# First operands made by engines alone, second pair loaded at the start, PE turning the identity meanwhile: an LSH attention and mixture-of-experts kernel on one core

## The chip, the cores and the metric

The kernel runs on one core of a Trainium2 chip. The metric is device time in microseconds (us) of one launch, as the median of several runs. The engines are named as the profile names them: PE (TensorE; PEld is its weight load), DVE (VectorE), ACT (ScalarE), POOL (GpSimd), and SP, whose queue issues most DMAs.

## What is computed

Inputs are q, k, v of 4 batches x 8 heads x 768 tokens x 64, a projection of 64 x 6, and the weights of 8 experts. Attention runs only inside a hash bucket; the rest of the kernel is a top-1 mixture of experts on the 3072 x 512 result.

```python
q_bits = (np.einsum('bhsd,dk->bhsk', q, proj) > 0)     # 6 sign bits per row; k likewise
mask = q_bucket[:, :, :, None] == k_bucket[:, :, None, :]
scores = np.where(mask, scale * np.matmul(q, k.transpose(0, 1, 3, 2)), -1000000000.0)
attn = np.exp(scores - max); attn = attn / (attn.sum + 1e-09)
x = np.matmul(attn, v)                                  # heads side by side: 3072 x 512
...
h = np.maximum(x[mask] @ w1[e], 0.0); ye = h @ w2[e]    # for the expert e with the largest logit
out[mask] = gate_w * sigmoid(x @ w_output_gate)[e] * ye
```

## The kernel before

Heads go in 16 pairs. A pair takes 12 steps, a step is one tile of 128 query rows of one head against all 768 keys, so there are 192 steps. `scores` (L476) does eight matmul rows per step: xl against xr (128 deep) and yl against yr (76 deep), each in two halves of 384 keys, into one of two PSUM buffers `ps_s`. The four operand tiles of a head hold a rounded value, its remainder, and the 12 sign bits that make the mask: xl and xr the rounded q and k with k's remainder, yl q's remainder and query bits, yr rounded k and key bits. DVE copies the masked scores out with their minimum (L488), ACT takes the exponential (`soft`, L496), DVE inverts the row sum (L503, L504), POOL scales (`normal`, L506), PE turns the result (`transposed`, L517), ACT copies it out (L518) and PE multiplies by v (`weighted`, L528).

The order on PE, DVE, ACT and POOL is the order of the code. Steps go in groups of two; a step's scaling comes two steps later, its transposes four, its products from step 10 on. The lists `at` and `products` hang extra work on steps: `plan(step, fn)`.

What makes the operands differs by pair. For the later pairs, `project` (L386) makes four small matmuls on the pair's two `qk` tiles and one DVE comparison into `bt`; `split_hi` (L430, POOL) rounds, `split_lo` (L438, DVE) takes remainders, and `spread` (L446) has SP issue eight DMAs per head that copy halves of these tiles between partitions: xr and yr from xl, xr from yl, xl from xl, and the bits from `bt` into yr and yl. For the first pair, head 0 is made by engines (`first_head`, L399), and head 1 by `project(0, (1,))`, `split_hi`, `split_lo` and `spread(..., True)`, whose large copies go to ACT and POOL and whose bits go by DMA. The projection operand `pjc` comes from `pj` by four small DVE instructions (L89, L90).

Before the first step the code issues: the two loads of pair 0, the identity (POOL), head 0, head 1, the first load of pair 1, the second, the load of v, and `more_constants` (L123), a list of 29 small POOL instructions and one DMA. Pair 1's `project` is planned for step 4, `split_hi` for steps 3 and 5, `split_lo` for 5 to 8, `spread` for 6 and 8. There are two buffers for `qk`. `tile_of` (L470) takes the three tiles of one head and then of the other in steps 0 to 5, and alternates heads afterwards.

After step 191 the kernel runs the experts, with PE as the busiest engine; nothing there is touched by the change.

Of the kernel before, what the change touches and what calls it, by code (L numbers as in the profile page):

```python
# [20 lines left out]
NB = 6  # L21
# [23 lines left out]
GROUP = 2  # L45
NFB = F // P
# [12 lines left out]
def lsh_attention_then_moe(  # L59
# [21 lines left out]
    pj = cst.tile([P, NB + 5], F32, name="pj")  # L81
    nc.scalar.dma_start(pj, proj)
    thr, scl, thr0, scl0, sgn = (pj[:, NB + i:NB + i + 1] for i in range(5))
    pjc = cst.tile([P, 32 + 2 * NB], F32, name="pjc")
    nc.vector.memset(pjc, 0.0)
    for h, s in ((0, 1.0), (1, -1.0)):
        hs = slice(h * D, (h + 1) * D)
        c = 2 * NB * h
        nc.vector.tensor_scalar(pjc[hs, c:c + NB], pj[hs, 0:NB], s, None, ALU.mult)  # L89
        nc.vector.tensor_scalar(pjc[hs, c + NB:c + 2 * NB], pj[hs, 0:NB], -s, None, ALU.mult)  # L90
# [32 lines left out]
    def more_constants():  # L123

        nc.gpsimd.memset(wgt, 0.0)
        nc.sync.dma_start(wgt[:, :, 0:2 * E], wgo.rearrange("(g p) c -> p g c", p=P))

# [6 lines left out]
        for ti, tf, pattern, first, cm in iotas:  # L134
            nc.gpsimd.iota(ti, pattern=pattern, base=first, channel_multiplier=cm)
            nc.gpsimd.tensor_copy(tf, ti)
        nc.gpsimd.memset(base, 0.0)
        for i, c in enumerate(CAPS):
            nc.gpsimd.memset(caps[:, i:i + 1], float(c))
        nc.gpsimd.memset(tacc_e, 0.0)  # L140
        for a in range(NB32):
            nc.gpsimd.memset(quart[32 * a:32 * a + 32], float(a))

# [209 lines left out]
    with ExitStack() as actx:  # L353
# [32 lines left out]
        def project(g, heads=(0, 1)):  # L386
            st = pairs[g]
            pp = ps_m.tile([P, HS], F32, name="ps_m")
            for j in heads:
                for n in range(2):  # L390
                    r = 32 * (2 * j + n)
                    nc.tensor.matmul(pp[r:r + 32], pjc[:, 0:32], st["qk"][j][:, n * HS:(n + 1) * HS],
                                     start=True, stop=True)
            bt = hp.tile([P, HS], F32R, name="bt", bufs=2)
            hs = slice(heads[0] * D, (heads[-1] + 1) * D)
            nc.vector.tensor_scalar(bt[hs], pp[hs], thr[hs], scl[hs], ALU.is_gt, ALU.mult)
            st["bt"] = bt

        def first_head():  # L399

            st = pairs[0]
            qk = st["qk"][0]
            xl, xr = (hp.tile([P, S], F32R, name=n) for n in ("xl", "xr"))
            yl = hp.tile([P, S], F32R, name="yl")
            yr = hp.tile([D + 2 * NB, S], F32R, name="yr")
            for k, t in (("xl", xl), ("yl", yl), ("xr", xr), ("yr", yr)):
                st[k] = [t, None]
            pp = ps_m.tile([P, HS], F32, name="ps_m")
            for m in range(2):
                ms = slice(m * D, (m + 1) * D)  # L410
                for n in range(2):
                    r = 32 * (2 * m + n)
                    nc.tensor.matmul(pp[r:r + 32], pjc[ms, 2 * NB * m:2 * NB * m + 32], qk[ms, n * HS:(n + 1) * HS],
                                     start=True, stop=True)
            nc.scalar.copy(xr[D:P], qk[D:P])
            nc.gpsimd.tensor_scalar(xr[0:D], qk[D:P], 1.0, 0.0, ALU.mult, ALU.add)
            nc.scalar.activation(xl[0:D], qk[0:D], AF.Copy, scale=-0.125)
            nc.vector.tensor_tensor(xr[D:P], qk[D:P], f32(xr[D:P]), ALU.subtract)
            nc.scalar.activation(xl[D:P], qk[0:D], AF.Copy, scale=-0.125)
            nc.gpsimd.tensor_scalar(yr[0:D], qk[D:P], 1.0, 0.0, ALU.mult, ALU.add)  # L420
            bt = hp.tile([P, HS], F32R, name="bt", bufs=2)
            nc.vector.tensor_scalar(bt, pp, thr0, scl0, ALU.is_gt, ALU.mult)
            nc.vector.scalar_tensor_tensor(yl[0:D], qk[0:D], -0.125, f32(xl[0:D]), ALU.mult, ALU.subtract)
            for n in range(2):
                cs = slice(n * HS, (n + 1) * HS)
                nc.gpsimd.tensor_scalar(yr[D:D + 2 * NB, cs], f32(bt[D + 32 * n:D + 32 * n + 2 * NB]), 1.0, 0.0,
                                        ALU.mult, ALU.add)
                nc.scalar.copy(yl[D:D + 2 * NB, cs], f32(bt[32 * n:32 * n + 2 * NB]))

        def split_hi(g, j):  # L430
# [3 lines left out]
            xl = hp.tile([P, S], F32R, name="xl")  # L434
# [11 lines left out]
        def spread(g, j, hurry=False):  # L446
# [5 lines left out]
            if hurry:  # L452
                qk = st["qk"][j]
                for t in ("xr", "yr"):
                    nc.scalar.copy(st[t][j][0:D], qk[D:P])
                nc.gpsimd.tensor_scalar(st["xr"][j][D:P], yl[D:P], 1.0, 0.0, ALU.mult, ALU.add)
                nc.scalar.activation(st["xl"][j][D:P], qk[0:D], AF.Copy, scale=-0.125)
            else:
                nc.sync.dma_start(xr[0:D], xl[D:P])
                nc.sync.dma_start(yr[0:D], xl[D:P])  # L460
                nc.sync.dma_start(xr[D:P], yl[D:P])
# [599 lines left out]
```

## Time and profile before

| | |
|---|---|
| median of 3 runs | 802.86 us (801.79 to 804.91) |
| the profiled execution | 803.36 us |
| its span, first to last instruction | 801.6 us |
| PE busy | 776.2 us, 97% |
| DVE, ACT, POOL busy | 59%, 57%, 47% |
| mean granted PE clock | 0.992 |

The profile describes one execution; 1.76 us of its time lie outside the span. Busy PE time is modelled from matmul ends, so a busy PE is not a PE at its peak. A row of the timeline has start, duration, engine, line, operation, result and sources, shape, count, and in brackets the idle time of that engine before it with what ended it.

### The profile page before, as it was taken

The page shows a single profiled execution, that of the slowest core. Times are in us where ns is not written, and L with a number is a line of the kernel's source. Part 1 is how long each engine was busy: PE and PEld are TensorE (multiplying, and loading weights), DVE is VectorE, ACT ScalarE, POOL GpSimd, SP SyncE. Part 2 cuts the span into 40 slices and gives each one's busy share as a digit, 9 for nine tenths or more (in the row PEclk, how much of TensorE's full clock was granted, in tenths as well). Part 3 has the DMA queues.
Part 4 walks back from the last instruction along what each step waited for, and adds up shares of the span by engine and source line. Part 5 has one row for each costly group of instructions (what it writes and reads, how often), then busy time and mean ns, then how long its engine had stood idle before and what let it go on. Part 6 is the DMA issues. An engine that isn't in the chain of part 4 may idle for free. (4 is left out here: it accounts for less than half of the span.)

```text
span 801.6 us, 13652 instructions
## 1 busy us (share of the span) xinstructions
PE 776.2 (97%) x4656; PEld 606.2 (76%) x4656; DVE 472.6 (59%) x1036; ACT 459.1 (57%) x934; POOL 375.9 (47%) x415
## 2 busy tenths in 40 slices
PE   6899999999999999999999999999999999999997
PEld 3666776667676667676667668888899999998895
DVE  5566676687666677667777546345444546454640
ACT  5767777657777667777677761144242525352331
POOL 5535444434534344544446864363617372746101
PEclk9999999999999999999999999999999999999999
DMA  3543645544655444564465512364444444444601
GB/s 123 127 110 77 146 89 127 135 97 91 144 125 103 105 127 81 125 145 87 110 154 145 146 28 67 132 202 152 148 131 154 151 151 148 147 150 164 226 27 38
DMA packets 84895, 98.94 MB, mean 123 GB/s; under 512 B 58047, under 2 KB 59535, under 8 KB 84816
## 3 DMA queue, kind: packets, MB, share of 16 engines
q1 hardware_dynamic: 79472, 84.66, 40.5%
q0 software_dynamic: 5200, 13.31, 4.9%
q8 instruction: 39, 0.64, 0.3%
q14 instruction: 40, 0.33, 0.1%
q10 hardware_dynamic: 144, 0.01, 0.0%
HBM read 59.48 MB, written 13.11 MB: 91 GB/s over the span
## 5 line engine op out<-in xcount | busy, mean ns | idle before, releaser
L506 POOL TENSOR_SCALAR sc<-sc,rsum 128x768 f32<-128x768 f32 x192 | 179.8, 948 | 234.6 <-DVE rsum L504 127.9
L488 DVE TENSOR_SCALAR_CACHE_REDUCE sc<-ps_s 128x768 f32<-128x768 f32 x192 | 183.4, 956 | 115.0 <-PE ps_s L484 105.9
L518 ACT COPY pts<-ps_t 128x384 f32<-128x384 f32 x384 | 164.3, 480 | 99.2 <-PE ps_t L517 98.6
L496 ACT ACTIVATE sc<-sc,mn 128x768 f32<-128x768 f32 x192 | 181.3, 944 | 25.2 <-DVE sc L488 16.2
L517 PE MATMUL ps_t<-ident,sc 128*128 128x128 f32 x1152 | 159.3, 274 | 4.9 <-POOL sc L506 2.4
L517 PEld LDWEIGHTS ps_t<-ident,sc 128*128 128x128 f32 x1152 | 136.7, 141 | 18.0 <-issue 6.7
L528 PE MATMUL ps_a<-pts,vt 128*64 128x384 f32 x768 | 148.6, 510 | 0.0
L484 PE MATMUL ps_s<-xr,xl 128*128 128x384 f32 x384 | 119.5, 393 | 5.2 <-DVE sc L488 3.3
L484 PEld LDWEIGHTS ps_s<-xr,xl 128*128 128x128 f32 x384 | 59.5, 195 | 78.5 <-issue 36.3
L484 PE MATMUL ps_s<-yr,yl 76*128 76x384 f32 x384 | 101.8, 347 | 0.2 <-issue 0.2
L297 PE MATMUL ps_s<-xh,w1h 128*128 128x256 f32 (+7 forms) x288 | 97.3, 338 | 2.1 <-DVE hl L308 1.6
L308 DVE SCALAR_TENSOR_TENSOR hl<-ps_s,hh 128x256 fp32r<-128x256 f32 (+8 forms) x40 | 34.0, 849 | 110.8 <-ACT hh L307 110.8
L297 PE MATMUL ps_s<-xlo,w1h 128*128 128x256 f32 (+7 forms) x288 | 95.4, 331 | 0.0
L297 PE MATMUL ps_s<-xh,w1l 128*128 128x256 f32 (+7 forms) x288 | 95.3, 331 | 0.0
L271 POOL DMA_INDIRECT xq<-x_dram,idx x75 | 81.6, 1088 | 21.6 <-issue 21.0
L528 PEld LDWEIGHTS ps_a<-pts,vt 128*64 128x64 f32 x768 | 47.5, 138 | 51.9 <-issue 50.1
L314 POOL DMA_INDIRECT out_dram<-yo,sid x29 | 30.6, 1057 | 115.3 <-ACT yo L313 61.3
L307 ACT ACTIVATE hh<-ps_s 128x256 fp32r<-128x256 f32 (+8 forms) x40 | 29.0, 726 | 92.8 <-PE ps_s L297 92.8
L484 PEld LDWEIGHTS ps_s<-yr,yl 76*128 76x128 f32 x384 | 72.0, 194 | 0.7 <-issue 0.5
L297 PEld LDWEIGHTS ps_s<-xh,w1h 128*128 128x128 f32 x288 | 54.2, 188 | 5.1 <-DVE hl L308 2.1
L297 PEld LDWEIGHTS ps_s<-xlo,w1h 128*128 128x128 f32 x288 | 54.2, 188 | 1.1
L297 PEld LDWEIGHTS ps_s<-xh,w1l 128*128 128x128 f32 x288 | 54.2, 188 | 1.1
(199 smaller groups left out, 1000.5 us busy)
## 6 DMA issues: line engine op xcount, KB each, us to landing
w_raw<-in_w_dram SPq DMA_DIRECT2D x36, 512.0 KB
qk<-in_qkT_dram SPq DMA_DIRECT2D x32, 384.0 KB
xh<-in_w_dram SPq DMA_DIRECT2D x14, 512.0 KB
xlo<-in_w_dram SPq DMA_DIRECT2D x14, 512.0 KB
vt<-in_v_dram SPq DMA_DIRECT2D x16, 384.0 KB
xr<-xl SPq DMA_DIRECT2D x30, 192.0 KB
yr<-xl SPq DMA_DIRECT2D x30, 192.0 KB
xr<-yl SPq DMA_DIRECT2D x30, 192.0 KB
```

Of the source, the lines that this page charges most:

```text
L271: nc.gpsimd.indirect_dma_start(out=xq[:, k * P:(k + 1) * P], out_offset=None, in_=x_dram.rearrange("n (a f) -> (n a) f", a=NB32), in_offse ...
L297: nc.tensor.matmul(ps, l, r, start=first and k == 0, stop=last and k == len(pairs) - 1)
L307: nc.scalar.activation(hh, ph, AF.Relu)
L308: return lambda: nc.vector.scalar_tensor_tensor(hl, ph, 0.0, f32(hh), ALU.max, ALU.subtract)
L314: nc.gpsimd.indirect_dma_start(out=out[:, :], out_offset=bass.IndirectOffsetOnAxis(ap=sid[0:n, r, a:a + 1], axis=0), in_=yo[0:n], in_offse ...
L484: nc.tensor.matmul(ss[:, n, 0:HS], l[0:k, qs], r[0:k, n * HS:(n + 1) * HS], start=first, stop=not first)
L488: nc.vector.tensor_scalar(sc, ss[:, :, 0:HS], MASKED, None, ALU.min, ALU.min, accum_out=mn)
L496: nc.scalar.activation(pr, pr, AF.Exp, bias=mn, scale=-1.0, accum_out=sums[s // GROUP][:, k:k + 1])
L506: nc.gpsimd.tensor_scalar(live[s0 + k], live[s0 + k], rs[:, k:k + 1], 0.0, ALU.mult, ALU.add)
L517: nc.tensor.transpose(tr[:, c], pr[:, (3 * h + c) * P:(3 * h + c + 1) * P], ident)
L518: nc.scalar.copy(pts[:, 3 * h:3 * h + 3, t * P:(t + 1) * P], tr)
L528: nc.tensor.matmul(st["av"][j * D:(j + 1) * D], st["v"][:, j, c], blocks[hb][j][:, c], start=(c == 0), stop=(c == NT - 1))
```

## The change

- `first_head` becomes `first_heads`: both heads of pair 0 are projected straight from `pj` (which now carries the projection twice, padded to 32 columns), each into its own PSUM tile, and all operands are made on POOL, ACT and DVE. No DMA carries bits for pair 0. The remainders of head 1 (`first_low`: four DVE instructions and one on POOL) stand after step 0, as do the four small instructions that make `pjc` (`signed`), now on POOL.
- Pair 1's two loads and the first load of v are issued at the start, and there are four `qk` buffers. Pair 1's project, split and spread come one step earlier. Steps 12 to 17 also take one head's three tiles and then the other's.
- PE turns the identity 14 times into a `ps_t` tile before its first projection.
- `more_constants` is cut into ten parts, planned for steps 18, 20, ... 36.

```diff
-    pj = cst.tile([P, NB + 5], F32, name="pj")
+    pj = cst.tile([P, 32 + 4], F32, name="pj")
...
-    def more_constants():
+    def gate_weights():
         nc.gpsimd.memset(wgt, 0.0)
         nc.sync.dma_start(wgt[:, :, 0:2 * E], wgo.rearrange("(g p) c -> p g c", p=P))
...
+    def more_constants():
+        return [gate_weights, triangle] + [lambda i=i: numbers(*i) for i in iotas] + [counters, tables]
...
-                t = hp.tile([P, S], F32, name="qk", bufs=2)
+                t = hp.tile([P, S], F32, name="qk", bufs=4)
...
+            pps = [ps_m.tile([P, HS], F32, name="ps_m"), ps_a.tile([P, HS], F32, name="ps_a")]
+            for j in range(2):
+                project_bits(j, pps[j])
+            nc.scalar.copy(xr[0][D:P], qk[0][D:P])
+            round_to(xr[0][0:D], qk[0][D:P])
+            nc.scalar.activation(xl[0][0:D], qk[0][0:D], AF.Copy, scale=-0.125)
+            nc.vector.tensor_tensor(xr[0][D:P], qk[0][D:P], f32(xr[0][D:P]), ALU.subtract)
+            nc.scalar.activation(xl[0][D:P], qk[0][0:D], AF.Copy, scale=-0.125)
+            round_to(yr[0][0:D], qk[0][D:P])
+            set_bits(pps[0])
+            split_hi(0, 1, xl[1])
+            nc.vector.scalar_tensor_tensor(yl[0][0:D], qk[0][0:D], -0.125, f32(xl[0][0:D]), ALU.mult, ALU.subtract)
+            key_bits(0)
+            query_bits(0)
+            set_bits(pps[1])
+            round_to(xr[1][0:D], qk[1][D:P])
+            key_bits(1)
+            query_bits(1)
+            nc.scalar.copy(yr[1][0:D], qk[1][D:P])
...
-            t, j = (i % 3, i // 3) if s < 6 else (i // 2, i % 2)
+            t, j = (i % 3, i // 3) if s // 6 in (0, 2) else (i // 2, i % 2)
...
-                s0 += 2 * (g == 1)
+                s0 += g == 1
...
+        for i, fn in enumerate(more_constants()):
+            plan(18 + 2 * i, fn)
...
             load(0)
+            load(1)
+            load_v(0)
             make_identity(nc, ident)
-            first_head()
-            project(0, (1,))
-            split_hi(0, 1)
-            split_lo(0, 1, 0)
-            split_lo(0, 1, 1)
-            load(1, (0,))
-            spread(0, 1, True)
-            load(1, (1,))
-            load_v(0)
-            more_constants()
+            warm = ps_t.tile([P, 3, P], F32, name="ps_t")
+            for i in range(NWARM):
+                nc.tensor.transpose(warm[:, i % 3], ident, ident)
+            first_heads()
...
+                    if s == 0:
+                        first_low()
+                        signed()
```

The order of POOL before, from pair 0's key bits on (`bt` holds the bits, `sc` is a step's scaled tile):

```order
L426 TENSOR_SCALAR yr<-bt 12x384 x2
L435 TENSOR_SCALAR xl<-qk,pj 128x768
L456 TENSOR_SCALAR xr<-yl 64x768
L125 MEMSET wgt 128x128
L129 MEMSET t_ob 128x128
L130 AFFINE_SELECT t_ob<-t_ob 128x128
L132 CAST tri<-t_ob 128x128
```

The same place in the change, with the lines numbered by the new code (L552 is `normal`):

```order
L439 TENSOR_SCALAR yr<-bt 12x384 x2
L449 TENSOR_SCALAR xr<-qk 64x768
L439 TENSOR_SCALAR yr<-bt 12x384 x2
L480 TENSOR_SCALAR xl<-qk 64x768
L93 TENSOR_SCALAR pjc<-pj 64x6
L94 TENSOR_SCALAR pjc<-pj 64x6
L552 TENSOR_SCALAR sc<-sc,rsum 128x768 x2
L488 TENSOR_SCALAR xl<-qk,pj 128x768
```

The rounding of head 1 now stands ahead of these rows, and the first scaling follows without the constants between.

The order of SP's queue before, from its start (L379 loads qk, L461 and L462 copy parts of pair 1's operands):

```order
L379 DMA qk<-in_qkT_dram 128x768 x2
L384 DMA vt<-in_v_dram 128x768 x2
L466 DMA yr<-bt 12x384
L379 DMA qk<-in_qkT_dram 128x768
L466 DMA yr<-bt 12x384
L467 DMA yl<-bt 12x384 x2
L379 DMA qk<-in_qkT_dram 128x768
L126 DMA wgt<-in_wgo_dram 128x4x16
L459 DMA xr<-xl 64x768
L460 DMA yr<-xl 64x768
L466 DMA yr<-bt 12x384 x2
```

And in the change, from its start:

```order
L394 DMA qk<-in_qkT_dram 128x768 x4
L399 DMA vt<-in_v_dram 128x768 x2
L394 DMA qk<-in_qkT_dram 128x768 x2
L512 DMA yr<-bt 12x384
L505 DMA xr<-xl 64x768
L506 DMA yr<-xl 64x768
L512 DMA yr<-bt 12x384
L507 DMA xr<-yl 64x768
L508 DMA xl<-xl 64x768
L505 DMA xr<-xl 64x768
L513 DMA yl<-bt 12x384 x2
```

The loads of pairs 0, 1 and 2 now all stand ahead of pair 1's copies; before, pair 2's loads stood among them.

## Rows read from the trace of the kernel before

**Rows 1.** The page's busy times: PE.
```profile
PE 776.2 (97%) x4656; PEld 606.2 (76%) x4656; DVE 472.6 (59%) x1036; ACT 459.1 (57%) x934; POOL 375.9 (47%) x415
```

**Rows 2.** Stretches: bounds, length, busy time of each engine, granted PE clock, DMA share, GB/s.
```profile
10.08:21.95 11.87, 10.20 (x36) 7.19 (x35) 7.07 (x17) 7.83 (x15) 9.63 (x39) 1.00 0.28 75
21.95:31.97 10.02, 9.59 (x63) 8.31 (x60) 8.94 (x20) 8.05 (x20) 5.20 (x6) 1.00 0.61 146
31.97:49.05 17.08, 14.95 (x85) 8.82 (x83) 7.59 (x20) 10.94 (x26) 7.35 (x9) 0.90 0.37 88
49.05:53.42 4.37, 4.37 (x30) 3.16 (x29) 4.06 (x11) 3.16 (x9) 1.91 (x2) 1.00 0.62 128
...
24.04:33.83 9.79, 9.25 (x64) 7.61 (x62) 9.28 (x23) 9.79 (x23) 4.68 (x5) 1.00 0.57 148
```

**Rows 3.** Timeline of PE, 0 to 25 us.
```profile
5.47 2.41 PE L413 MATMUL ps_m<-qk,pjc 64*32 64x384 f32 x8 [5.47 <-DVE pjc L90]
...
19.04 1.54 PE L517 MATMUL ps_t<-ident,sc 128*128 128x128 f32 x6 [1.03 <-POOL sc L506]
20.51 1.51 PE L392 MATMUL ps_m<-qk,pjc 128*32 128x384 f32 x8
21.95 1.01 PE L484 MATMUL ps_s<-xr,xl 128*128 128x384 f32 x2
...
23.40 0.78 PE L517 MATMUL ps_t<-ident,sc 128*128 128x128 f32 x5
...
24.04 0.60 PE L484 MATMUL ps_s<-xr,xl 128*128 128x384 f32 x2
...
24.83 0.82 PE L517 MATMUL ps_t<-ident,sc 128*128 128x128 f32 x6
```

**Rows 4.** Timeline of DVE, 4 to 13 us.
```profile
4.62 0.74 DVE L89 TENSOR_SCALAR pjc<-pj 64x6 f32<-64x6 f32 x1 [3.63 <-DMA pj<-in_proj_dram]
...
7.93 0.68 DVE L422 TENSOR_SCALAR bt<-ps_m,pj 128x384 fp32r<-128x384 f32 x1 [0.73 <-PE ps_m L413]
...
11.46 1.15 DVE L443 SCALAR_TENSOR_TENSOR yl<-qk,pj,xl 128x384 fp32r<-128x384 f32 x2 [0.57 <-POOL xl L435]
12.64 0.96 DVE L488 TENSOR_SCALAR_CACHE_REDUCE sc<-ps_s 128x768 f32<-128x768 f32 x1
```

**Rows 5.** POOL: timeline to 20 us, between it L426's instructions (ns min/median/max).
```profile
1.08 0.29 POOL masks.py:199 TENSOR_SCALAR_AFFINE_SELECT ident<-ident 128x128 f32<-128x128 f32 x1
...
L426 POOL TENSOR_SCALAR yr<-bt x2: 508/828/1147, 8.7 to 9.9; 12x384 fp32r<-12x384 f32 x2
...
13.65 0.20 POOL L125 MEMSET wgt<- 128x128 f32 x1
...
14.67 0.20 POOL L133 MEMSET ones<- 128x128 bf16 x1
...
17.50 0.48 POOL L142 MEMSET quart<- 32x1 f32 x4
18.08 1.79 POOL L506 TENSOR_SCALAR sc<-sc,rsum 128x768 f32<-128x768 f32 x2
```

**Rows 6.** Timeline of SP's queue and PE, 35 to 46 us.
```profile
35.79 0.47 SPq L462 DMA_DIRECT2D xl<-xl  x1
...
38.74 0.58 PE L484 MATMUL ps_s<-xr,xl 128*128 128x384 f32 x2 [1.84 <-DMA xl<-xl]
...
40.71 2.83 PE L528 MATMUL ps_a<-pts,vt 128*64 128x384 f32 x8
...
45.27 0.85 PE L392 MATMUL ps_m<-qk,pjc 128*32 128x384 f32 x8
```

**Rows 7.** Timeline of POOL, 55 to 58 us.
```profile
55.87 1.98 POOL L506 TENSOR_SCALAR sc<-sc,rsum 128x768 f32<-128x768 f32 x2 [2.38 <-PE ps_s L484]
```

**Rows 8.** Two later stretches, columns as in rows 2.
```profile
150.00:175.00 25.00, 23.50 (x148) 15.66 (x145) 20.61 (x61) 15.19 (x37) 10.10 (x10) 0.93 0.43 89
...
275.00:300.00 25.00, 23.50 (x147) 15.55 (x145) 20.55 (x61) 15.43 (x35) 10.27 (x11) 0.93 0.41 104
```

More of the change, by code (lines that the diff above doesn't have):

```diff
@@ L133, in more_constants, with numbers, counters @@
         nc.gpsimd.memset(ones, 1.0)
-        for ti, tf, pattern, first, cm in iotas:
-            nc.gpsimd.iota(ti, pattern=pattern, base=first, channel_multiplier=cm)
-            nc.gpsimd.tensor_copy(tf, ti)
+    def numbers(ti, tf, pattern, first, cm):
+        nc.gpsimd.iota(ti, pattern=pattern, base=first, channel_multiplier=cm)
+        nc.gpsimd.tensor_copy(tf, ti)
+    def counters():
         nc.gpsimd.memset(base, 0.0)
@@ L393, in project, with first_heads @@
                                      start=True, stop=True)
             bt = hp.tile([P, HS], F32R, name="bt", bufs=2)
-            hs = slice(heads[0] * D, (heads[-1] + 1) * D)
-            nc.vector.tensor_scalar(bt[hs], pp[hs], thr[hs], scl[hs], ALU.is_gt, ALU.mult)
+            nc.vector.tensor_scalar(bt, pp, thr, scl, ALU.is_gt, ALU.mult)
             st["bt"] = bt
-        def first_head():
+        def first_heads():
             st = pairs[0]
[L402 to L410, printed above, removed]
-                for n in range(2):
[L412 to L423, printed above, removed]
@@ new lines, in first_heads, with project_bits @@
+            qk = st["qk"]
+            for k in ("xl", "yl", "xr"):
+                st[k] = [hp.tile([P, S], F32R, name=k) for _ in range(2)]
+            st["yr"] = [hp.tile([D + 2 * NB, S], F32R, name="yr") for _ in range(2)]
+            xl, yl, xr, yr = (st[k] for k in ("xl", "yl", "xr", "yr"))
+            bits = []
+            def project_bits(j, pp):
+                for m in range(2):
+                    ms = slice(m * D, (m + 1) * D)
+                    for n in range(2):
+                        r = 32 * (2 * m + n)
+                        nc.tensor.matmul(pp[r:r + 32], pj[ms, 0:32], qk[j][ms, n * HS:(n + 1) * HS],
+                                         start=True, stop=True)
@@ new lines, in set_bits, with key_bits @@
+            def set_bits(pp):
+                bt = hp.tile([P, HS], F32R, name="bt", bufs=2)
+                nc.vector.tensor_scalar(bt, pp, 0.0, set0, ALU.is_gt, ALU.is_equal)
+                bits.append(f32(bt))
+            def key_bits(j):
+                for n in range(2):
+                    r = D + 32 * n
+                    nc.gpsimd.tensor_scalar(yr[j][D:D + 2 * NB, n * HS:(n + 1) * HS], bits[j][r:r + 2 * NB], 1.0, 0.0,
+                                            ALU.mult, ALU.add)
@@ new lines, in query_bits, with round_to @@
+            def query_bits(j):
+                for n in range(2):
+                    r = 32 * n
+                    nc.scalar.activation(yl[j][D:D + 2 * NB, n * HS:(n + 1) * HS], bits[j][r:r + 2 * NB], AF.Copy,
+                                         scale=PEN)
+            def round_to(dst, src):
+                nc.gpsimd.tensor_scalar(dst, src, 1.0, 0.0, ALU.mult, ALU.add)
+            pps = [ps_m.tile([P, HS], F32, name="ps_m"), ps_a.tile([P, HS], F32, name="ps_a")]
+            for j in range(2):
+                project_bits(j, pps[j])
@@ L433, in split_hi @@
                 st.setdefault(k, [None, None])
[L434 removed]
+            if xl is None:
+                xl = hp.tile([P, S], F32R, name="xl")
             nc.gpsimd.tensor_scalar(xl, st["qk"][j], sgn, 0.0, ALU.mult, ALU.add)
@@ L451, in spread @@
             xr, yr = f32(st["xr"][j]), f32(st["yr"][j])
[L452 to L461, printed above, removed]
-                nc.sync.dma_start(xl[D:P], xl[0:D])
+            nc.sync.dma_start(xr[0:D], xl[D:P])
+            nc.sync.dma_start(yr[0:D], xl[D:P])
+            nc.sync.dma_start(xr[D:P], yl[D:P])
+            nc.sync.dma_start(xl[D:P], xl[0:D])
             for n in range(2):
```

46 lines of the change are left out of this document (26 added, 20 removed).

## The prediction, written before the changed kernel was timed

> **What bounds the kernel now.** I read the page's busy times first: PE is busy for 776 us, 97% of the span [rows 1]. So a change off PE gains only where PE waits, or runs slowly. I then cut the span into stretches at places where PE begins the scores of a certain step, counting the score rows on PE's timeline: step 0 at 10.08, step 5 at 21.95, step 11 at 31.97, step 16 at 49.05 us [rows 2, 3]. From step 16 on two steps take 4.37 us with PE full [rows 2]. That is the pace of the rest of the attention, so what happens after step 16 only moves with it, and the question is how much earlier step 16 begins. Three stretches come before it.
>
> *Start to step 5.* PE waits until 5.47 us for DVE's preparation of `pjc` [rows 3], which itself waited until 4.62 for the small load of `pj` [rows 4]. POOL's list of constants runs from 13.65 to about 17.98, and the first scaling begins right behind it at 18.08 [rows 5]; PE had waited 1.03 us for that at 19.04 [rows 3]. And PE runs slowly here. The clock column prints 1.00 [rows 2], but the durations contradict it: a score pair takes 1.01 us at 21.95 and 0.60 us at 24.04; six transposes take 1.54 us at 19.04 and 0.82 us at 24.83 [rows 3]. [...]
>
> *Steps 5 to 11.* Six steps in 10.02 us, 1.67 each [rows 2]. ACT is busy for all of 24.04 to 33.83 (9.79 of 9.79 us) [rows 2]: with no products yet, ACT's exponential and copies set the pace, not PE.
>
> *Steps 11 to 16.* 17.08 us for five steps [rows 2]. PE waits 1.84 us at 38.74 for the copy `xl<-xl` of pair 1, issued only at 35.79 [rows 6]; then the granted clock falls (0.90 over the stretch [rows 2]) and eight product rows take 2.83 us [rows 6].
>
> **The change, part by part.** The sum is made against the profiled execution, 803.36 us (span 801.6 and 1.76 around it); it lies 0.50 us above the median of the runs.
>
> *Step 5.* The projections no longer wait for `pjc`: they need `pj` (4.62, [rows 4]) and PE, which has turned the identity 14 times. POOL has made the identity by 1.08 + 0.29 = 1.4 us [rows 5], and one transpose at the low level is 1.54/6 = 0.26 us [rows 3], so PE is free at 1.4 + 14 x 0.26 = 5.0. These transposes cost nothing of their own but 0.4 us: `pj` isn't there before 4.62. Head 0's projection (1.5 us, as at 20.51 [rows 3]) ends at about 6.6, the comparison (0.68, [rows 4]) at 7.3. The key bits on POOL come next: the two such instructions lasted 0.51 and 1.15 us [rows 5], so they end between 8.4 and 9.6; I take 8.9. Step 0's scores then finish at about 9.5, and DVE copies them out from 9.6, 3.0 us earlier than at 12.64 [rows 4]. Most of that is given back at once: `first_low` puts four half-tile DVE instructions behind it, 4 x 1.15/2 = 2.3 us by the nearest row [rows 4], so step 1's copy begins at 9.6 + 0.9 + 2.3 = 12.8 and ends at 13.7, which frees the buffer for step 3's scores. `first_low`'s own results are needed for step 3 as well, so both come in time together. The POOL rounding `xl` and the four small `pjc` instructions follow beside step 2; the first scaling after them. With the constants gone it is bound by the row sum, after step 2's copy (about 15.0), and done at 15.9. PE from 13.8: scores of step 3, pair 1's projection, scores of step 4, transposes of step 0, then step 5. At the high level, from start to next start, a score step is 24.83 - 24.04 = 0.79, a projection nearly the 0.85 of 45.27 [rows 6], six transposes some 0.6 (0.82 with the last one's tail [rows 3]): 0.8 + 0.8 + 0.8 + 0.6 = 3.0, so step 5 begins at 16.8. At the low level these are 1.45 (21.95 to 23.40), 1.45 (20.51 to 21.95), 1.45 and 1.47 (19.04 to 20.51) [rows 3]: 5.8, and step 5 at 19.6. Against 21.95 that is a gain of 5.1 or of 2.3 us. I take 5.0: PE is busy without a gap from 1.4 to about 8, longer than the gapless stretch from 19.04 that ended in the rise at 23.4, and slow scores before step 2 cost little, since DVE sets that part.
>
> [...] The trace shows the rise at 23.4 after a gapless run of transposes, projection and scores from 19.04 [rows 3], so it can't say which of them brought it. [...]
>
> *Steps 5 to 11.* ACT's work per step is unchanged, so 10.0 us again. Gain 0.
>
> *Steps 11 to 16.* Pair 1's tiles are loaded at the start, so the splits wait for nothing but their turn, and SP's queue has no load of pair 2 between the copies (it stands ahead, and needs only pair 0's buffers, free by about 14). The last remainder of head 0 follows step 5's copy, at about 19.5; its copies and bits, two DMA hops that each took up to 2.95 us before (35.79 to 38.74, [rows 6]) plus issues, end near 26.5, and step 12 begins near 30.2. Head 1's come some 4 to 5 us later, and the new tile order asks for them only at step 15, near 36. So both waits go. Without them: the first step with products 3.3 us (1.67 for a step and two products at some 1.44 to 1.5), then two groups at 4.37 [rows 2], and pair 2's projection, 0.8: 12.8 us. The gain is 17.1 - 12.8 = 4.3, with the slow stretch after the wait included. If head 1's copies were late by as much as one such wait, 1.84 us [rows 6], it would be 2.5.
>
> *Costs moved later.* The ten parts of the constants take 4.3 us of POOL together, the largest (`triangle`) 13.8 to 14.9, 1.1 us [rows 5]. POOL idles 2.38 us before each scaling in the steady steps [rows 7], waiting for others; with a `split_hi` of 0.9 in the same group the largest part still fits. I cost it at nothing; if that cover were gone, the whole of it is 4.3 us. The gate weights' DMA waits for a POOL instruction of step 18, with pair 2's last copies behind it on SP; those are needed from step 24, some 13 us later. Nothing. More loads at the start (six of 384 KB instead of four) stand behind pair 0's own in the queue, and the small load of `pj` met a busy queue before too; 0 to 0.5 us, and I take 0.
>
> Sum: 5.0 + 0 + 4.3 = 9.3 less 0.1 for the unknowns above, 9.2 us: 803.36 - 9.2 = **794.2 us**, 8.7 below the median of the runs. The bounds of the terms (2.3 to 5.1, and 2.5 to 4.3, and key bits 0.5 either way) give gains of 4.5 to 10, so its own range is 792.5 to 797.
>
> **The rivals.**
> - *The clock stays low, or falls again, until step 5.* For: no row shows the clock rise behind transposes alone [rows 3], and PE still waits from about 10.5 to 13.7 for `first_low` and step 1's copy, 3 us, where before a wait of 1.84 us with little work around it was followed by the low clock [rows 6]. Against: 6.5 us of gapless work. Gain 2.3 + 4.3 = 6.6: 796.8 us. [...]
> - *The change does not bring pair 1 in time.* The DMA copies still follow one another in pairs on one queue, with larger loads in flight. If head 0 or head 1 stalls as before, only step 5's gain is left: 803.4 - 4.6 = 798.8. Against: 4 us of slack for either head by the working above.
> - *Later slow stretches fall away.* At 150 to 175 and 275 to 300 us the clock averages 0.93 over 25 us [rows 8]: 25 x 0.07 x 2 = 3.5 us at half speed, 1.75 us lost each. PE waits there anyway, and all moves 9 us earlier; if the clock didn't follow those waits this time, both losses go: 794.2 - 3.5 = 790.7. A third such stretch would as well add 1.75.
> - *Slower than before.* The ten constant parts sit in steps 18 to 36, where PE has no slack. Should a part stand ahead of a scaling that PE waits for, PE waits and the clock falls after it, 1.75 us each as just worked out. Ten times that and the 4.3 us of the parts are 21.8 us: 794.2 + 21.8 = 816. It decides where a part is longer than POOL's idle time, 2.38 us less 0.9 in a group with a split [rows 7]; the longest is 1.1. So it is unlikely.
>
> **How the numbers follow.** Forecast 0.55, low clock 0.22, pair 1 late 0.08, later slow stretches gone 0.12, slower 0.03. From 790.5 to 798 all cases but the third, the last and some tails of the rest are held, about 8 in 10. A measurement of this kernel tells about 0.5%, 4.0 us, from no change, so faster means under 798.8: the first, second and fourth case and half of the third, 0.93; no change 0.04; slower 0.03.
>
> **What would show it.** In the changed profile: PE busy from about 1.4 us with 14 transposes of some 0.26 us, the first scores at about 8 us; step 1's copy on DVE behind the four `first_low` instructions near 12.8; the first scaling near 15.0; step 5 at 16.8 (19.6 with the low clock); ACT full between steps 5 and 11; no wait of PE on `xl<-xl` or `yl<-bt` at steps 12 to 15; step 16 near 39.8; then 4.37 us per two steps. The prediction is wrong if step 16 comes after 44, if PE's scores at step 12 or 15 wait for a DMA, if PE waits for POOL in steps 20 to 40, or if the attention's later pace changes.

## The result, and the profile after

The changed kernel takes 799.03 us as the median of 11 runs (796.41 to 799.68), the kernel before 802.86 us beside it (11 runs, 799.76 to 804.91). The ratio is 0.9949, 95% interval 0.9934 to 0.9964. That is a gain of 3.8 us, where 8.7 were forecast and the range, 790.5 to 798 us, began at 4.9: the prediction is **wrong in size**, right in sign. Three of the eleven runs took 796.4 to 797.0 us at a mean granted clock of 0.992 to 0.995, the other eight 798.7 to 799.7 at 0.986 to 0.990; the profiled execution is one of the eight (799.08 us, span 797.4). Against the profile before it gains 803.36 - 799.08 = 4.28 us.

The page's busy times of the changed kernel (before: [rows 1]):

```profile
PE 772.7 (97%) x4674; PEld 606.8 (76%) x4674; DVE 472.4 (59%) x1034; ACT 458.4 (57%) x934; POOL 383.4 (48%) x422
```

Its stretches between the same steps (step 0 to 5, 5 to 11, 11 to 16, 16 to 18), columns as in [rows 2], where the four that answer to these stand:

```profile
6.81:19.96 13.15, 9.62 (x35) 6.48 (x35) 8.88 (x18) 6.95 (x14) 9.09 (x14) 0.61 0.34 116
19.96:30.20 10.24, 9.10 (x63) 7.58 (x62) 10.01 (x24) 9.76 (x23) 7.01 (x7) 1.00 0.56 128
30.20:43.19 12.99, 12.87 (x85) 8.25 (x84) 7.27 (x18) 10.83 (x26) 7.18 (x9) 1.00 0.50 128
43.19:47.55 4.36, 4.36 (x30) 3.18 (x28) 4.06 (x11) 3.15 (x9) 1.91 (x2) 1.00 0.51 106
```

The reader sees three things. Steps 11 to 16 shrank from 17.08 to 12.99 us, at a clock of 1.00 instead of 0.90. Steps 5 to 11 kept their length. But step 5 begins at 19.96 instead of 21.95, and the clock of the first stretch is 0.61. PE's timeline tells why (start, duration, operation; in brackets the idle time before and what ended it):

```profile
1.43 3.25 PE L833 MATMUL ps_t<-ident 128*128 128x128 f32 x14 [1.43 <-POOL ident masks.py:199]
4.61 1.45 PE L428 MATMUL ps_m<-qk,pj 64*32 64x384 f32 x8
5.89 0.82 PE L428 MATMUL ps_a<-qk,pj 64*32 64x384 f32 x8
6.81 0.58 PE L530 MATMUL ps_s<-xr,xl 128*128 128x384 f32 x2
9.03 1.28 PE L530 MATMUL ps_s<-yr,yl 76*128 76x384 f32 x2 [1.65 <-POOL yr L439]
10.11 0.84 PE L530 MATMUL ps_s<-xr,xl 128*128 128x384 f32 x2
...
14.80 0.98 PE L530 MATMUL ps_s<-xr,xl 128*128 128x384 f32 x2 [1.78 <-DVE sc L534]
...
16.35 1.51 PE L407 MATMUL ps_m<-qk,pjc 128*32 128x384 f32 x8
17.79 1.01 PE L530 MATMUL ps_s<-xr,xl 128*128 128x384 f32 x2
...
19.24 0.96 PE L563 MATMUL ps_t<-ident,sc 128*128 128x128 f32 x6
19.96 0.60 PE L530 MATMUL ps_s<-xr,xl 128*128 128x384 f32 x2
```

A score pair is the two `xl` by `xr` rows of a step, which has two `yl` by `yr` rows besides. The clock did rise early, by the durations (its column prints 1.00 from the start to 9.28): the second projection takes 0.82 us (the first 1.45), the first score pair 0.58. Then PE waits 1.65 us for the key bits, which come at 9.03; the granted clock falls to 0.50 at 9.29, and the next projection takes 1.51 us, a score pair 1.01: PE is back at the low clock, 0.50 in the column, until 19.5. The low level below means durations like these last two, the high level a projection of 0.85 us and a score pair of 0.6. POOL and DVE show what the wait stood behind:

```profile
4.29 0.83 POOL L449 TENSOR_SCALAR xr<-qk 64x768 fp32r<-64x768 f32 x1 [2.91 <-DMA qk<-in_qkT_dram]
5.20 1.45 POOL L449 TENSOR_SCALAR yr<-qk 64x768 fp32r<-64x768 f32 x1
6.75 1.64 POOL L488 TENSOR_SCALAR xl<-qk,pj 128x768 fp32r<-128x768 f32 x1
8.48 1.09 POOL L439 TENSOR_SCALAR yr<-bt 12x384 fp32r<-12x384 f32 x2
```

```profile
5.00 0.95 DVE L457 TENSOR_TENSOR xr<-qk,xr 64x768 fp32r<-64x768 f32 x1 [4.04 <-ACT xr L454]
6.14 0.62 DVE L433 TENSOR_SCALAR bt<-ps_m,pj 128x384 fp32r<-128x384 f32 x1 [0.18 <-PE ps_m L428]
6.68 0.94 DVE L462 SCALAR_TENSOR_TENSOR yl<-qk,xl 64x768 fp32r<-64x768 f32 x1
...
10.35 0.96 DVE L534 TENSOR_SCALAR_CACHE_REDUCE sc<-ps_s 128x768 f32<-128x768 f32 x1 [2.21 <-PE ps_s L530]
...
13.70 0.94 DVE L534 TENSOR_SCALAR_CACHE_REDUCE sc<-ps_s 128x768 f32<-128x768 f32 x1
```

DVE had the bits `bt` ready at 6.76, but the rounding `xl` of head 1 stood ahead on POOL, so the key bits began at 8.48. Step 0's copy followed at 10.35, step 1's at 13.70.

Much of the rest of the loss lies far behind, in the last expert but one. ACT, POOL and PE there, and two stretches across it:

```profile
730.30 0.69 ACT L328 ACTIVATE yo<-ps_m,tacc 128x512 f32<-128x512 f32 x1 [12.45 <-DMA out_dram<-yo,sid]
```

```profile
727.41 1.03 POOL L329 DMA_INDIRECT out_dram<-yo,sid  x1 [0.30 <-issue]
```

```profile
732.68 0.49 PE L312 MATMUL ps_s<-xh,w1h 128*128 128x368 f32 x1 [1.99 <-DVE hl L323]
732.96 0.51 PE L312 MATMUL ps_s<-xlo,w1h 128*128 128x368 f32 x1
...
736.51 0.33 PE L312 MATMUL ps_s<-xlo,w1h 128*128 128x368 f32 x1
```

```profile
732.00:735.00 3.00, 2.32 (x8) 2.33 (x9) 2.99 (x4) 3.00 (x4) 0.17 (x2) 0.65 0.30 94
735.00:738.00 3.00, 3.00 (x16) 3.00 (x15) 3.00 (x3) 1.11 (x2) 0.87 (x1) 0.78 0.92 283
```

PE waits 1.99 us for DVE's `hl`, DVE for ACT's `hh`, and ACT has its `yo` ahead of that, which waits for the scatter of the `yo` two before (two buffers), and POOL issued that scatter only at 727.41, behind gathers. After the wait the clock is low (0.65 and 0.78, and 0.50 from 732.92 to 736.33). In the kernel before the same place stands 6.16 us later and the clock stays up (1.00 from 738.00 to 745.00):

```profile
738.84 0.44 PE L297 MATMUL ps_s<-xh,w1h 128*128 128x368 f32 x1 [1.57 <-DVE hl L308]
...
741.12 0.33 PE L297 MATMUL ps_s<-xlo,w1h 128*128 128x368 f32 x1
```

The rows at 736.51 and 741.12 are the same product, the fourteenth counted from 732.68 and 738.84. The lead over the kernel before is 6.16 us at the first of them and 4.61 at the fourteenth: the stretch of low clock (732.92 to 736.33 us) costs 1.55 us.

So the lead over the kernel before, by the starts on PE, is 1.99 us at step 5, 1.8 at step 11, 5.87 at step 16, 7.10 at step 188 (456.54 against 463.64), 6.16 behind that wait, 4.61 behind the low clock, and 4.28 at the end.

### The profile page after: what moved, and what is told of

The parts are those of the page before. It is cut to its first block, busy times and chain, and to the rows that moved or that the text cites. A ratio compares the mean times of both kernels' runs of the same rounds, so it can differ in the third digit from the quotient of the medians.

```text
span 797.4 us, 13687 instructions
## 1 busy us (share of the span) xinstructions
PE 772.7 (97%) x4674; PEld 606.8 (76%) x4674; DVE 472.4 (59%) x1034; ACT 458.4 (57%) x934; POOL 383.4 (48%) x422
## 5 line engine op out<-in xcount | busy, mean ns | idle before, releaser
L552 POOL TENSOR_SCALAR sc<-sc,rsum 128x768 f32<-128x768 f32 x192 | 180.4, 953 | 224.2 <-DVE rsum L550 116.1
L542 ACT ACTIVATE sc<-sc,mn 128x768 f32<-128x768 f32 x192 | 181.3, 944 | 28.7 <-DVE sc L534 19.5
L574 PE MATMUL ps_a<-pts,vt 128*64 128x384 f32 x768 | 144.8, 499 | 0.0
```

The costliest lines, as they stand in the source:

```text
L542: nc.scalar.activation(pr, pr, AF.Exp, bias=mn, scale=-1.0, accum_out=sums[s // GROUP][:, k:k + 1])
L552: nc.gpsimd.tensor_scalar(live[s0 + k], live[s0 + k], rs[:, k:k + 1], 0.0, ALU.mult, ALU.add)
L574: nc.tensor.matmul(st["av"][j * D:(j + 1) * D], st["v"][:, j, c], blocks[hb][j][:, c], start=(c == 0), stop=(c == NT - 1))
```

## The experiments

Each run has its own row of numbers here; a lead is the kernel's time before less its own, from the profiles, at the start of step 16, of step 188, and at the end. The last column is the difference of the two before it. Ratios are to runs of the kernel before on the same chip (802.25 us for e1 to e4, 803.37 for e6 to e9). All leads are against the one profile of the kernel before, so each carries the scatter of two single executions; the eleven runs of the kernel before lie between 799.8 and 804.9 us.

| run | ratio (95% interval) | step 5 | lead 16 | lead 188 | lead at end | given back |
|---|---|---|---|---|---|---|
| the change | 0.9949 (0.9934 to 0.9964) | 19.96 | 5.87 | 7.10 | 4.28 | 2.8 |
| e1_swap | 0.9920 (0.9891 to 0.9948) | 19.48 | 6.65 | 7.45 | 5.17 | 2.3 |
| e2_nowarm | 0.9930 (0.9906 to 0.9955) | 19.19 | 6.52 | 7.84 | 6.03 | 1.8 |
| e3_fill | 0.9912 (0.9877 to 0.9947) | 17.58 | 7.70 | 8.63 | 5.91 | 2.7 |
| e4_loads | 0.9935 (0.9908 to 0.9962) | 20.74 | 5.42 | 5.80 | 6.00 | -0.2 |
| e6_low_later | 0.9948 (0.9930 to 0.9966) | 17.48 | 8.21 | 9.07 | 3.39 | 5.7 |
| e7_no_loads | 0.9993 (0.9979 to 1.0008) | 19.69 | 2.97 | 4.29 | 1.51 | 2.8 |
| e8_const_only | 0.9970 (0.9950 to 0.9991) | 20.36 | 0.39 | 0.81 | 0.20 | 0.6 |
| e9_loads_const | 0.9940 (0.9921 to 0.9959) | 20.23 | 5.53 | 5.95 | 5.85 | 0.1 |

**Is it the wait for the key bits?** The rounding of head 1 behind the bits of head 0:

```diff
-            split_hi(0, 1, xl[1])
...
             key_bits(0)
+            split_hi(0, 1, xl[1])
```

> The changed kernel, but POOL makes head 0's key bits before it rounds head 1's tile, not after. Theory A (PE's wait of 1.65 us for the key bits let the clock fall at about 9.6 us, and the low clock then holds step 5 back to 19.96): the wait shrinks to 0.5 us or less, step 0's second operand pair starts near 7.5 instead of 9.03; if the clock stays high through the later wait for the remainders of head 1, step 5 begins near 17, total about 796; if that later wait lets it fall, step 5 comes near 19. Theory B (DVE's and POOL's chain sets step 5 whatever the clock): step 0 comes 1 us or more earlier, the rounding of head 1 comes as much later, and step 5 stays within 0.5 us of 19.96.

The wait fell from 1.65 to 0.51 us, and the clock fell only at 12.6 instead of 9.3 us. Step 5 came at 19.48, 0.5 us earlier: the low clock moved to the next wait of PE, 2.96 us before step 3's scores at 14.00, and still covered what precedes step 5 (a score pair of 0.98 us at 14.00, a projection of 1.51 at 15.55).

**Do the transposes do anything?** The change without them.

```diff
-            warm = ps_t.tile([P, 3, P], F32, name="ps_t")
-            for i in range(NWARM):
-                nc.tensor.transpose(warm[:, i % 3], ident, ident)
```

> The changed kernel without the 14 transposes of the identity. Theory A: the clock was low again from 9.6 to 19.6 us in the changed kernel, so the transposes bought only quicker second projection and first score pair, under 1 us, of which most is lost in the wait for the key bits: step 5 within 0.7 us of 19.96 and total within 1 us of the changed kernel. Rival: the transposes carry the gain at the start (the first scores at 6.81 against 10.08): without them step 5 comes 1.5 us or more later, total 800.5 or more.

Step 5 came at 19.19, no later than with them, so in this kernel the 14 transposes buy nothing. PE's first projections took 1.50 us each here, the first score pair 1.01. So the early rise in the changed kernel was theirs, and it was lost behind the wait. Without them the clock rose later (a score pair of 0.51 us at 9.67) and fell at 11.55, ahead of PE's wait of 2.38 us for DVE that ended at 14.37.

**What does the low clock cost at step 5?** The change, with idle transposes of the identity where PE waits: 16 ahead of step 0, 6 ahead of step 2, 24 ahead of step 3.

```diff
+FILL = {0: 16, 2: 6, 3: 24}
...
+                    if s in FILL:
+                        turn_idle(FILL[s])
```

> The changed kernel with more transposes of the identity where PE waits in the first steps: 16 before step 0, 6 before step 2, 24 before step 3. They compute nothing that is used. Theory A (the low clock costs step 5 its time): transposes stay at about 0.1 us each, the score pairs of steps 1 to 5 last 0.6 us instead of 0.84 to 1.01, and step 5 begins near 17.5, 2.4 us earlier; total near 796.5. Theory B (DVE and POOL set step 5): the clock may stay high, but step 5 stays within 0.7 us of 19.96, total within 1 us of the changed kernel's 799.0.

PE's timeline:

```profile
1.43 3.15 PE L834 MATMUL ps_t<-ident 128*128 128x128 f32 x14 [1.43 <-POOL ident masks.py:199]
4.51 0.85 PE L429 MATMUL ps_m<-qk,pj 64*32 64x384 f32 x8
...
5.94 1.97 PE L840 MATMUL ps_t<-ident 128*128 128x128 f32 x16
...
11.83 2.79 PE L840 MATMUL ps_t<-ident 128*128 128x128 f32 x24
14.46 0.58 PE L531 MATMUL ps_s<-xr,xl 128*128 128x384 f32 x2
...
15.32 0.85 PE L408 MATMUL ps_m<-qk,pjc 128*32 128x384 f32 x8
...
17.58 0.59 PE L531 MATMUL ps_s<-xr,xl 128*128 128x384 f32 x2
```

From 4.51 us on all of it runs at the high level: a projection 0.85 us, a score pair 0.58. Step 3 began little earlier (14.46 against 14.80, behind DVE), step 5 2.4 us earlier. So 2.4 of the 3.0 us missing at step 5 are the clock. Here 14 transposes alone, the first thing PE did, were followed by a projection at the high level, 0.85 us. The same holds in e14_after_again (the unaltered change, once more):

```profile
1.43 3.07 PE L833 MATMUL ps_t<-ident 128*128 128x128 f32 x14 [1.43 <-POOL ident masks.py:199]
5.08 0.85 PE L428 MATMUL ps_m<-qk,pj 64*32 64x384 f32 x8 [0.58 <-DMA pj<-in_proj_dram]
```

But the rise did not come at the same moment each time. In e6_low_later (below) both projections behind the same 14 transposes were slow:

```profile
4.61 1.51 PE L429 MATMUL ps_m<-qk,pj 64*32 64x384 f32 x8
5.89 1.50 PE L429 MATMUL ps_a<-qk,pj 64*32 64x384 f32 x8
```

The clock was up by 4.5 us in e3, by 5.9 in the change and by 7.4 in e6 (the eight idle transposes there took 1.18 us).

**Which part carries the gain?** First the early loads in the kernel before (loads of pair 1 and v at the start, four `qk` buffers, pair 1 one step earlier, the tile order of steps 12 to 17), then the change without them.

```diff
-                t = hp.tile([P, S], F32, name="qk", bufs=2)
+                t = hp.tile([P, S], F32, name="qk", bufs=4)
...
-                s0 += 2 * (g == 1)
+                s0 += g == 1
...
+            load(1)
+            load_v(0)
```

> The kernel before with one part of the change alone: pair 1's two loads and v at the start, four qk buffers, pair 1's work one step earlier, steps 12 to 17 by head. Theory A (this part is worth steps 11 to 16, 17.08 us before and 12.99 in the changed kernel): step 5 stays near 21.95, steps 11 to 16 take 13 us, step 16 near 45, total about 799. Rival (the part needs the others, since POOL still makes the constants ahead of pair 1's splits and SP still carries pair 0's bits): PE waits again for pair 1's copies in steps 12 to 15, gain under 2 us, total 801 or more.

The stretch from step 11 to step 16, columns as above:

```profile
30.65:43.64 12.99, 12.86 (x86) 8.24 (x84) 7.54 (x20) 10.82 (x26) 7.19 (x9) 1.00 0.48 124
```

This part alone has the gain of the whole change: steps 11 to 16 in 12.99 us, 797.36 us as the median, the ratio within the interval of the whole.

> The changed kernel without its second part: pair 1 loaded after the first heads, two qk buffers, pair 1's work in the old steps, heads alternating from step 6. Theory (the early loads carry the gain after step 11): PE waits for pair 1's copies again, steps 11 to 16 take 16 to 17 us instead of 12.99, step 16 comes at 46.5 to 48, total 801 or more, a gain under 1.5 us. Rival (without the constants ahead of its splits pair 1 is in time anyway): steps 11 to 16 take under 14 us, total 799 to 800.

Steps 11 to 16 took 16.89 us, with the wait of the kernel before back in its place, here on PE:

```profile
36.22 0.98 PE L530 MATMUL ps_s<-xr,xl 128*128 128x384 f32 x2 [2.12 <-DMA xl<-xl]
```

The time was that of the kernel before. That is less than the row of starts says: step 16 and step 188 began 3.0 and 4.3 us earlier, and 2.8 us of this went in the experts.

**The constants alone, and both parts together without the new first pair.** The ten parts in the kernel before; then these and the early loads.

> The kernel before with the constants alone cut into ten parts and planned for steps 18 to 36. Theory (they held the first scaling from about 16.65 to 18.08, and PE behind it): step 5 comes 1 to 1.5 us earlier than 21.95, but pair 1's copies are still late, so step 16 comes 0 to 1.5 us earlier than 49.05; steps 18 to 40 keep 4.37 us per two steps; total 801.5 to 803. Rival (POOL's parts cost the later steps): the pace in steps 18 to 40 falls, total above 803.4.

Step 5 came 1.6 us earlier (20.36), but PE then waited 1.85 us on `xl<-xl` before 37.23, and step 16 came 0.4 us earlier. The median is 801.40 us, 2.0 below the kernel before, which these rows do not explain: the profiled execution, 803.16 us, is the second slowest of ten that reach from 797.0 to 803.2.

> The kernel before with both the early loads (as in e4_loads) and the constants in ten parts: everything of the change but the engine-made first pair and the 14 transposes. Theory (the new first pair gives back what it gains, so these two parts are the whole change): step 5 near 19.5 to 20, step 16 near 42.5 to 43, total within 1 us of the changed kernel. Rival (the engine-made first pair earns 1.5 us or more): step 16 at 44.5 or later, total 1.5 us above the changed kernel or more.

Step 16 at 43.53, within 0.4 us of the whole change (43.19), and 797.57 us. The engine-made first pair and the transposes therefore earn 0.3 us at step 16, and nothing that shows at the end.

**More lead at the start.** The swap, idle transposes (8, 6 and 12), and `first_low` one step later:

```diff
-                    if s == 0:
+                    if s == 1:
                         first_low()
```

> The changed kernel with head 0's key bits ahead of head 1's rounding (as in e1_swap), with transposes of the identity in PE's waits (8 before step 0, 6 before step 2, 12 before step 3; they compute nothing that is used), and with the remainders of head 1 behind step 1's copy on DVE, not ahead of it. Theory (with the clock high, what is left at step 5 is DVE's chain, in which the four remainder instructions stand ahead of step 1's copy): step 3 starts near 13.2 instead of 14.5 in e3_fill, step 5 near 16.5 instead of 17.58, step 16 near 40.3. Rival (the scaling of steps 0 and 1, or ACT, sets step 5): step 5 stays within 0.3 us of 17.58.

Step 3 came at 14.34, not sooner, since its scores then waited 1.77 us for POOL's remainder `xl`, which `first_low` itself makes. Lead 9.07 at step 188, the largest of all, and 3.39 at the end: PE waited 3.17 us at the place near 732, and the clock stayed low for twice as long as in the changed kernel (0.82 over 728 to 733 us, 0.50 over 733 to 738).

**The wait in the experts.** The column "given back" falls in two groups, by one execution each. Where a stretch of low clock stands near 732 to 740 us (the change, e1, e3, e6, e7; a product there takes 0.51 us instead of 0.33) it is 2.3 us or more. Where none stands there (e2, e4, e8, e9) it is 1.8 us or less. Read product against product with the kernel before, as above, the low clock takes 1.5 to 1.6 us in the change, e1, e3 and e7, and 2.5 in e6. The length of the wait alone does not decide whether it comes: 1.96 us in e2 was not followed by it, 1.88 in e3 was. e9 has the shortest wait and the clock up (1.00 from 730 to 740):

```profile
732.92 0.43 PE L308 MATMUL ps_s<-xh,w1h 128*128 128x368 f32 x1 [0.83 <-DVE hl L319]
```

The first try was to remove the wait: four buffers for `yo`, in the change, in the kernel before, and in two of the versions above.

```diff
-        yo = mp.tile([CH, DM], F32, name="yo", bufs=2)
+        yo = mp.tile([CH, DM], F32, name="yo", bufs=4)
```

> The changed kernel with four buffers instead of two for the expert output tile yo, so that ScalarE's yo no longer waits some 12 us for the scatter of the yo two before it. Theory (the late wait gives the lead back): in the last-but-one expert TensorE's wait for VectorE's hl falls from 1.99 us to under 0.8, no stretch of the low clock follows near 733 us, and the time is 796.0 to 797.3 (1.8 to 3 below the changed kernel's 799.03), with most executions near the lower of the two levels that the changed kernel showed. Rival (the wait has another owner, GpSimd's train of gathers or the arrival of weights): TensorE still waits 1.5 us or more within 10 us of that place, and the time stays within 1 us of 799.0.

> The kernel before with the same four buffers for yo: the control. Theory: the wait there, 1.57 us before 738.84 us in the kernel before, goes too, but no low clock followed it, so this gains 0.8 to 1.6 us: 801.3 to 802.1. If it gains as much as the changed kernel does (2 to 3 us), the buffers are a separate saving and do not explain what the changed kernel gave back. Rival: within 0.5 us of 802.86.

> The changed kernel with the idle transposes that kept the clock high in the first twenty us (796.21 as a median before) and four yo buffers. Theory: step 16 near 41.4 as before, the wait near 730 us gone, so the lead of some 8 us at the end of the routing reaches the end: 793.5 to 795.0. Rival: 796 or more, since the lead is lost elsewhere in the experts.

> The kernel before with the early loads and the constants in ten parts, without the engine-made first pair and the transposes (797.57 as a median before), and four yo buffers. Its profile showed a late wait of only 0.83 us and no low clock behind it, so the theory gives it a small gain: 796.4 to 797.3. If it gains 2 us or more, the yo buffers save something other than the wait and the clock behind it.

Ratios 0.9877 (0.985 to 0.9903), 0.9962 (0.9946 to 0.9978), 0.9857 (0.9836 to 0.9879) and 0.9891 (0.9865 to 0.9917). The wait and the low clock near 733 were gone from the profiles. But the kernel before took 808.51 us on this chip, and ACT showed waits of 3 to 7 us for which the profiles name no instruction, so the times were taken again, with the unaltered change in the same set:

> The changed kernel as it is, on the same chip and beside the same runs of the kernel before as the next three. Both theories: 0.993 to 0.997 of the kernel before, as the first time (0.9949), with the wait of about 2 us at the last-but-one expert's 128x368 products.

> The changed kernel with four yo buffers, once more. Theory (the wait for the scatter and the low clock behind it give the lead back): 1.5 to 3.0 us below the changed kernel as it is in this same set. Rival (the part gained in the last set, 0.9877 against 0.9949, belonged to a chip on which the kernel before took 808.5 us): within 1 us of it.

> The kernel before with four yo buffers, once more. Theory: 0.3 to 1.6 us below the kernel before, less than the buffers give the changed kernel. Rival: as much as there, and then the buffers are a saving of their own and the change's loss in the experts has another cause.

> The changed kernel with the idle transposes and four yo buffers, once more. Theory: 2 to 3 us below the changed kernel with the four buffers alone, as step 5 begins 2.4 us earlier, so 6.5 to 9 us below the kernel before. Rival: within 1 us of the changed kernel with four buffers, since the experts take the lead back in another wait.

The kernel before took 806.93 us, with the buffers 804.14 (0.9962, 0.9945 to 0.9979); the change 801.07 (0.9916, 0.989 to 0.9942), with them 799.32 (0.9892, 0.9865 to 0.9918). So they save 2.8 us in the one and 1.8 in the other, which the intervals do not tell apart: a saving of their own. The wait stands in both (1.57 us in the kernel before at first, 1.52 in the unaltered change here), so **the theory that the wait itself is what the change gave back falls**. The low clock behind the wait is not tested by these sets: in the profile of the unaltered change here the clock stayed at 1.00 behind it, and its low stretch in the experts stood at 546.9 to 550.3 us (0.50 over 548 to 550). The version with both gave 797.17 us (0.9872, 0.9847 to 0.9897), 9.8 below the kernel before, the most of this set (11 in the set before), and its profiled execution 794.79.

Then the wait was left and only filled, with 16 idle transposes in front of the products at 732.68, in the change and in e3_fill:

```diff
+IDLE = 16
...
+                if r == 6 and fp == 2:
+                    idle = ps_t.tile([P, 3, P], F32, name="ps_t")
+                    for i in range(IDLE):
+                        nc.tensor.transpose(idle[:, i % 3], ident, ident)
                 up(w1s, xs, hs, [2 * fp, 2 * fp + 1], n)()
```

> The changed kernel with 16 idle transposes of the identity on TensorE (0.12 us each by the idle ones already run) in the last-but-one expert, in front of the products that waited 1.99 us before 732.68 us; the wait itself stays. Theory (a wait of that length there is followed by the low clock, which costs 1.4 to 1.9 us): the idle turns fill the wait, no low clock follows near 733 us, and the median falls to the lower of the two levels of the changed kernel, 796.4 to 797.2, on a chip on which the kernel before takes 802 to 804. Rival (the low clock there does not depend on what TensorE does in the wait): 798.5 to 799.7 as before. On the chip on which the kernel before takes 807 to 808.5 the low clock stood elsewhere, and both expect no difference from the changed kernel.

> The same 16 idle transposes in the version with the idle transposes of the first steps (796.21 as a median, its wait there 1.88 us with the low clock behind it). Theory: both losses gone, step 5 near 17.6, 793.5 to 795.0 on a chip on which the kernel before takes 802 to 804. Rival: 795.7 or more, as without them.

PE's timeline of the first, and two stretches over the place:

```profile
732.97 1.91 PE L971 MATMUL ps_t<-ident 128*128 128x128 f32 x16
734.98 0.44 PE L313 MATMUL ps_s<-xh,w1h 128*128 128x368 f32 x1
735.25 0.33 PE L313 MATMUL ps_s<-xlo,w1h 128*128 128x368 f32 x1
```

```profile
732.00:735.00 3.00, 2.90 (x24) 2.63 (x22) 1.00 (x2) 2.40 (x4) 1.05 (x2) 1.00 0.11 36
735.00:738.00 3.00, 3.00 (x18) 3.00 (x19) 3.00 (x3) 3.00 (x4) 0.83 (x1) 1.00 0.45 132
```

The clock stays at 1.00, a product takes 0.33 us instead of 0.51. Lined up with the changed kernel's profile, this one stood 2.3 us behind it at these products and 0.8 us behind a few microseconds later: 1.5 us came back at the place. The medians do not show it: 801.18 us (0.9924, 0.9906 to 0.9943) and 798.70 (0.9895, 0.9875 to 0.9916), on a chip where the kernel before took 807.99 us. And in e14, on another such chip, the unaltered change had no low clock near 733 either. So what the low clock costs there is shown, 1.5 us; whether the idle transposes kept it away is not.

## Why the prediction was wrong

**The step that failed is "Step 5", its term "I take 5.0".** It measured 2.0 us. The reason given was that PE is busy without a gap from 1.4 to about 8. The rise came within that stretch, as said, and the clock was up by 5.9 (a projection of 0.82 us). But the working then has PE wait for the key bits, until 8.9, and its first rival has it wait from about 10.5 to 13.7 for `first_low`; the term still prices the 3.0 us before step 5 at the high level. The clock fell at 9.29, 0.26 us after the first of these waits. The other end of the term, 2.3 us with step 5 at 19.6, was the right one (19.96). The key bits came inside their bounds (8.4 to 9.6 forecast; the second ended at 9.57), but by luck: the comparison was done 0.5 us sooner than forecast (6.76 against 7.3), and the rounding `xl` of head 1, 1.64 us on POOL ahead of them, is not in the working. Step 1's copy was forecast for 12.8 and began at 13.70, hence 14.80 for step 3 where 13.8 was forecast. With the clock held up the same order gives 17.58 for step 5: 16.8 was 0.8 too early, 2.4 is the clock.

**Steps 5 to 11**, 0: 10.24 against 10.02 us, a loss of 0.2. **Steps 11 to 16**, 12.8 us: 12.99, no wait on a copy left, as said, and this is the whole lasting gain (e4, e7). **Costs moved later**, 0, as said: in steps 18 to 36, where the constants went, the lead does not shrink (5.87 us at step 16, 5.92 at step 40). Moving them alone brought step 5 forward by 1.6 us, since the scaling no longer stood behind them, but without the early loads pair 1 took that back.

**What was not in the sum.** **The second step that failed is "what happens after step 16 only moves with it".** With 2.0 in the place of 5.0 the sum would have been 797.2 us; another 1.6 us went behind step 16. Up to step 188 the lead grew by 1.2 us: 0.4 at 150 to 175 us and 0.4 at 275 to 300, where before the clock was 0.93 [rows 8] and this profile shows no low clock, and the rest little by little:

```profile
150.00:175.00 25.00, 22.51 (x153) 15.71 (x152) 21.14 (x64) 15.40 (x35) 9.23 (x10) 1.00 0.43 108
275.00:300.00 25.00, 22.50 (x148) 15.65 (x145) 17.79 (x51) 17.67 (x41) 11.14 (x12) 1.00 0.53 122
```

That is the third rival, worth 0.4 us a stretch where it was priced at 1.75 (the half speed in that price is the 0.50 that the clock column of the kernel before prints from 40.71 to 43.50 us). And it is no property of the kernel: in e14 the unaltered change shows 0.93 in both stretches. Then 2.8 us were given back: 0.95 up to the products at 732.68, as waits of PE grew (0.78 us against 0.48 at 484 us, 1.06 against 0.69 at 503, 1.99 against 1.57 at 732), 1.55 in the low clock behind them, and 0.3 behind the products, close to the end. The sum of the pieces, from step 5 on, is 2.0 - 0.2 + 4.1 + 1.2 - 2.8 = 4.3 us, the gain of the profiles.

**The range and the signs.** Gains of 4.5 to 10 us from 803.36 are 793.4 to 798.9 us, not the 792.5 to 797 that the working writes beside them; 799.03 lies just outside both. None of the four things that were to show the prediction wrong happened: step 16 came at 43.19, before 44; PE's scores at steps 12 and 15 waited for no DMA; PE waited for POOL nowhere in steps 20 to 40; and two steps still took 4.36 us. They watched neither the clock at step 5, short of a delay of 4 us, nor anything behind the attention.

**The rivals.** The first one happened at step 5: clock low, 796.8 us. The three runs at 796.4 to 797.0 sit on its number, which supports nothing: the rival has no growth and no loss behind step 16. The eight others are 2 us above. Their mean clock is lower by some 0.005, which over 797 us is, by estimate, 8 us more at 0.50; stretches of 3.4 us as near 733 would make two or three of them, and one such has cost 0.4 to 1.6 us here, so they are large enough for these 2 us. Only one of the eleven executions has a profile, so which stretches separate the two groups stays open. Pair 1 was in time, and no constant part delayed a scaling.

## What to carry to other kernels

Price work behind a wait at the clock that the wait leaves, not at the clock that the work before it earned; the stretch from step 3 to step 5 took 5.2 us here, at 0.50 up to 19.5 us, and 3.1 in e3 with the clock held up. Before making the start of a pipeline faster, look which later transfer sets the pace: here pair 1's early loads, with the buffers and the order that go with them, had the whole gain alone, and the elaborate engine-made first pair added nothing that shows. And a lead is not safe until the end: follow it stage by stage in both profiles. Here 3.4 us at 0.50 stood behind a wait of 1.99 us near 733 us, where the kernel before, after 1.57 us, kept 1.00.

## What was unexpected on the hardware

- The clock stayed up where idle transposes stood in PE's first waits: in e3_fill, with 14 + 16 + 6 + 24 of them, at about 0.12 us each once the clock is up, PE was at the high level from 4.5 us on. In e17 and e19, with the same ones, the column prints 1.00 from 0 to 26 us; in e14, e15 and e18, with the first 14 alone, 0.50 from 12 to 20. In e18 16 of them stood in the wait near 733 us and the clock stayed up (1.00 from 732 to 738), but it did so in e14 without them.
- Two POOL instructions ran long in the change, both beside DVE ones: the same 64x768 rounding took 0.83 us at 4.29, nearly alone, and again at 9.65, with DVE idle until 10.35, but 1.45 us at 5.20, where DVE's `xr<-qk,xr` began at 5.00. The rounding `xl` at 6.75, beside DVE's `yl<-qk,xl` at 6.68, took 1.64 us, and the same instruction 0.90 at 18.09, beside DVE's `bt<-ps_m,pj` at 18.03. What made the two long is not shown.
- On the chips of the last three sets (e10 to e19) ACT waited longer in the experts than in the earlier profiles, and the kernel before took 4 to 6 us more. One instruction of ACT in the first profile of the change, where the wait is for PE, and in that of the unaltered change there:

```profile
537.95 0.95 ACT L322 ACTIVATE hh<-ps_s 128x928 fp32r<-128x928 f32 x1 [4.32 <-PE ps_s L312]
```

```profile
543.63 0.94 ACT L322 ACTIVATE hh<-ps_s 128x928 fp32r<-128x928 f32 x1 [6.42 <-remote]
```

The profile names no instruction that ended the second wait. On such a chip the change gained 5.9 us instead of 3.8, and why is open.
